# Mish in pieces on GpSimd, V scaled by one product there, two buffers for O, and a new order of the work, in a kernel that mixes attention with a feed-forward branch

## The chip, the core and the metric

The kernel runs on one core of a Trainium2 chip. The core has five engines that run independently and meet at semaphores: TensorE (PE, matrix products; PEld is its loading of weights), VectorE (DVE), ScalarE (ACT), GpSimd (POOL) and SyncE (SP, which only issues transfers here). Each engine works through its own list of instructions in order. The metric is the time on the device in microseconds (us); a measurement is the median of several runs.

## The reference

Two branches work on the same x of 2048 tokens and 640 features, all in bfloat16, and a gate mixes them:

```python
g = _sigmoid((x * gate_w).sum(-1, keepdims=True))
# A: 32 heads of 20, softmax over 2048 keys
p = _softmax(einsum("bhqd,bhkd->bhqk", q, k) * Dh ** -0.5)
a = einsum("bhqk,bhkd->bhqd", p, v) ... @ wo
# B: 640 -> 1536 -> 640 with Mish
h = einsum("bsd,df->bsf", x, w1) + b1
sp = log1p(exp(-abs(h))) + where(h > 0, h, 0)
b = einsum("bsf,fd->bsd", h * tanh(sp), w2)
return g * a + (1 - g) * b
```

The largest piece of elementwise work is the exponential of 32 x 2048 x 2048 scores.

## The kernel before

**Attention.** Heads are taken in 8 groups of 4 (their 20 dimensions padded to 32 partitions, so that four heads use the four row blocks of TensorE). Queries are taken in 4 chunks of 512, keys in 16 tiles of 128. A block is one head, one key tile and one query chunk: 128x512 scores, of which there are 2048. Scores come out with the keys on the partitions (`score_mms`, L1219), so that the exponentials can go straight into the product with V, which has a column of ones ahead of it for the sum (`pv`, L1456).

**Two engines make exponentials.** In each step ScalarE takes two blocks, or three when a bank of PSUM is spare, in one instruction (`emit_e`, L1246). Beside that VectorE takes whole tiles (four heads of one key tile, `emit_x`). For each of the four blocks one instruction scales the scores from PSUM into 16-bit integers that, read as float16, are an approximate exponential (L1304). Two more instructions add a constant to the whole 128x2048 tile (L1334), which gives two shifted copies, the shades. The product with V is then made three times, once with each shade, where the V of the second and third is scaled by 161/128 and 203/128. Those scaled V come from GpSimd: two products of 128x84 for each tile (`weigh`, L1359), kept in `VS`, which has 8 sets.

**End of a group of heads.** When all keys of a group and chunk are through, VectorE copies the accumulator to `OUNG` (L1551). SyncE moves the row of sums into `RR`, VectorE takes its reciprocal (L1558), SyncE writes it to DRAM and reads it back spread over the partitions into `BCT` (L1559, L1561), and GpSimd multiplies `OUNG` by `BCT` in four pieces of 128 columns (`times`, L1518). There is one `OUNG`.

**The feed-forward branch** runs between the steps of the attention as single tasks for TensorE (all through the helper `quarters`, L508): `h_task` makes x w1 (48 of them, VectorE adds the bias, L989), `mish` follows each second one (24 times, on 128x1024), `b_task` makes the product with w2, `p_task` that with wo. Mish is one Tanh on ScalarE (L1013), which gives U, and then six instructions on VectorE that compute a polynomial in U and multiply it by h:

```python
piece(FULL, lambda e: e.tensor_scalar(A, U, LIFT, LIFT, ALU.mult, ALU.add), taken)   # L1033
piece(SCALED, lambda e: e.tensor_scalar(B, A, 1 / LIFT, a - 2, ALU.mult, ALU.add))   # L1034
piece(FULL, lambda e: e.tensor_tensor(A, A, B, ALU.mult))                            # L1035
piece(SCALED, lambda e: e.tensor_scalar(B, A, 1 / LIFT, b - c, ALU.mult, ALU.add))   # L1036
piece(FULL, lambda e: e.tensor_tensor(A, A, B, ALU.mult))                            # L1037
piece(FULL, lambda e: e.tensor_tensor(h, A, h, ALU.mult), done)                      # L1038
```

U, A and B have one buffer each, so the next Mish waits for this one.

**What sets the order.** Nothing on the chip decides an order: a planner in Python (`Plan` and the loop at the end of `attention`) writes every engine's list when the kernel is built. It keeps an estimated time for each engine from constants in microseconds (`SHADE`, `TIMES`, `MISH` and others), emits one ScalarE step after the other, and fits the rest in: `start_tile` gives VectorE a new tile when VectorE is not too far behind, `pick` chooses a task for TensorE by its due step, `work` chooses the next instruction of VectorE from the queues `norm`, `soon` (shades), `blend` (Mish) and `bg`. Some twenty thresholds (`AHEAD`, `CROWD`, `XLATE`, `OVER` and others) steer this, and `STRETCHES` gives them other values for 35 stretches of steps. A transfer is taken as landed after an estimated time plus a margin (`safe`); GpSimd's products of O enter its list only then (`lasting`).

**The start.** SyncE loads the first chunk of x as rows, issues the transposing loads of chunks 1 and 2, then the three large blocks of wk, wq and wv, and then the transposing load of chunk 3.

Of the kernel before, what the change touches and what calls it, by code (L numbers as in the profile page):

```python
# [8 lines left out]
FP32 = mybir.dt.float32  # L9
# [8 lines left out]
P = 128  # L18
# [6 lines left out]
HG = 4  # L25
# [34 lines left out]
HALVED = 0.41  # L60
# [7 lines left out]
Q_WAIT = 6  # L68
# [7 lines left out]
TIMES = 0.7  # L76
# [13 lines left out]
MISH = 1.7  # L90
# [4 lines left out]
FULL = 0.60  # L95
SCALED = 0.34
LIFT = 512.0
FMIN = 0.109
# [12 lines left out]
CALM = 6  # L111
PACKED = 17
# [18 lines left out]
SETS = 8  # L131
ULPS = 1024 / math.log(2)
BASE = 13680.1
SHADE = 0.61
# [3 lines left out]
    13: {"EAGER": 144, "FMIN": 0.128, "FREE": 0.235, "SPUN": 0.495, "THIRD": 1.187, "VMIN": 1.48},  # L138
    33: {"EAGER": 144, "FMIN": 0.273, "FREE": 0.235, "SPUN": 0.495, "THIRD": 1.187, "VMIN": 1.48},
    53: {"CALLED": 7.573, "CALM": 3, "EAGER": 144, "FMIN": 0.332, "FREE": 0.235, "PATIENCE": 11.967, "ROOM": 2.116, "SPUN": 0.495, "THIRD": 1.187, "VMIN": 1.48, "XLATE": 10.107, "XSLACK": 0.076},  # L140
    74: {"AHEAD": 32, "CALLED": 7.573, "CALM": 8, "CROWD": 1.442, "EAGER": 144, "FMIN": 0.354, "FREE": 0.235, "NEED": 2, "OVER": 0.266, "PATIENCE": 3.941, "ROOM": 2.116, "SPUN": 0.467, "THIRD": 1.341, "VMIN": 1.48, "XLATE": 10.107, "XSLACK": 0.076},
    95: {"BUSY": 1.495, "CALLED": 2.701, "CROWD": 1.338, "FMIN": 0.33, "FREE": 0.173, "SPUN": 0.564, "STREAM": 0.496},
    116: {"CROWD": 1.454, "ROOM": 1.78, "STREAM": 0.464, "VMIN": 0.691, "XSLACK": 0.385},
    138: {"CROWD": 1.454, "EAGER": 159, "FREE": 0.15, "ROOM": 1.78, "STREAM": 0.464, "THIRD": 0.562, "VMIN": 0.691, "XSLACK": 0.385},
    159: {"XSLACK": 0.541},
    178: {"AHEAD": 13, "BEHIND": 21.412, "BUSY": 0.268, "CROWD": 1.246, "EAGER": 144, "FREE": 0.235, "MARGIN": 1.043, "OVER": 0.25, "PATIENCE": 12.851, "ROOM": 2.303, "XSLACK": 0.56},
    197: {"AHEAD": 17, "BEHIND": 13.21, "BUSY": 0.268, "CALLED": 2.332, "CALM": 9, "CROWD": 1.378, "EAGER": 144, "FMIN": 0.062, "FREE": 0.148, "LATER": 0.62, "MARGIN": 1.043, "OVER": 0.279, "PATIENCE": 8.968, "ROOM": 2.303, "XSLACK": 0.56},
    218: {"AHEAD": 17, "BEHIND": 13.21, "BUSY": 0.268, "CALLED": 2.332, "CALM": 9, "CROWD": 1.378, "EAGER": 156, "FMIN": 0.062, "FREE": 0.148, "KEPT": 14, "LATER": 0.62, "LOAD": 0.609, "MARGIN": 1.043, "OVER": 0.279, "PATIENCE": 13.444, "ROOM": 2.078, "STREAM": 0.365, "XLATE": 7.955, "XSLACK": 0.633},
    238: {"BUSY": 0.481, "EAGER": 131, "FMIN": 0.093, "LATER": 0.493, "LOAD": 0.49, "MARGIN": 0.871, "ROOM": 2.374, "XSLACK": 0.42},
    259: {"BUSY": 0.481, "CALLED": 1.571, "EAGER": 131, "FMIN": 0.065, "LATER": 0.493, "LOAD": 0.49, "MARGIN": 0.871, "NEED": 4, "OVER": 0.166, "ROOM": 2.345, "STREAM": 0.348, "VMIN": 2.036, "XSLACK": 0.42},  # L150
    279: {"AHEAD": 30, "BEHIND": 33.473, "BUSY": 0.531, "CALLED": 8.822, "CROWD": 1.719, "EAGER": 49, "FMIN": 0.065, "FREE": 0.217, "LATER": 0.531, "LOAD": 0.503, "MARGIN": 0.871, "NEED": 4, "OVER": 0.04, "ROOM": 2.185, "SLACK": 0.145, "SPARED": 1, "SPUN": 0.561, "STREAM": 0.574, "THIRD": 0.656, "VMIN": 2.036, "XSLACK": 0.539},
    301: {"AHEAD": 27, "BEHIND": 24.076, "BUSY": 0.655, "CALM": 8, "EAGER": 142, "FMIN": 0.157, "LATER": 0.445, "OVER": 0.136, "PATIENCE": 8.709, "ROOM": 3.21, "SLACK": 0.301},
    321: {"AHEAD": 27, "BEHIND": 24.076, "BUSY": 0.848, "CALM": 8, "EAGER": 125, "FMIN": 0.14, "FREE": 0.019, "LATER": 0.819, "MARGIN": 0.538, "OVER": 0.165, "PATIENCE": 7.178, "ROOM": 3.21, "SLACK": 0.301, "SPUN": 0.703, "THIRD": 0.853, "VMIN": 1.553, "XLATE": 6.963, "XSLACK": 0.575},
    343: {"OVER": 0.166},
    364: {},
    384: {"CALM": 5, "FREE": 0.144, "KEPT": 11, "OVER": 0.173, "XSLACK": 0.648},
    403: {"CALM": 5, "FREE": 0.072, "KEPT": 11, "OVER": 0.173, "SPARED": 2, "SPUN": 0.633, "XSLACK": 0.648},
    423: {"BEHIND": 10.627, "BUSY": 0.528, "CALLED": 3.206, "CALM": 5, "FREE": 0.072, "KEPT": 11, "MARGIN": 0.884, "OVER": 0.08, "PATIENCE": 6.789, "SPARED": 2, "SPUN": 0.633, "STREAM": 0.464, "XSLACK": 0.648},
    444: {"BUSY": 0.764, "CALLED": 6.746, "CALM": 5, "EAGER": 164, "FREE": 0.117, "MARGIN": -0.093, "OVER": 0.013, "THIRD": 1.182, "XLATE": 8.239},
    465: {"BEHIND": 11.273, "BUSY": 0.764, "CALLED": 6.746, "CALM": 5, "EAGER": 164, "FREE": 0.117, "LATER": 0.604, "MARGIN": -0.093, "OVER": 0.013, "ROOM": 1.536, "THIRD": 1.182, "VMIN": 0.904, "XLATE": 8.239},  # L160
    486: {"EAGER": 119, "OVER": 0.217, "SPARED": 2, "THIRD": 0.385},
    507: {"AHEAD": 48, "EAGER": 119, "OVER": 0.217, "SPARED": 1, "THIRD": 0.385, "VMIN": 1.003},
    527: {},
    546: {"OVER": 0.225, "ROOM": 1.348},
    566: {"BUSY": 1.219, "CALLED": 3.326, "FREE": 0.185, "LATER": 0.559, "LOAD": 0.591, "NEED": 4, "OVER": 0.225, "ROOM": 1.348, "SPUN": 0.456, "THIRD": 0.564},
    585: {"BUSY": 1.219, "CALLED": 2.639, "FREE": 0.185, "LATER": 0.559, "LOAD": 0.591, "NEED": 4, "OVER": 0.142, "ROOM": 1.696, "SLACK": 0.273, "SPUN": 0.533, "THIRD": 0.564, "XSLACK": 0.639},
    606: {"BUSY": 1.219, "CALLED": 2.639, "FREE": 0.185, "LATER": 0.559, "LOAD": 0.591, "NEED": 4, "OVER": 0.142, "PATIENCE": 3.342, "ROOM": 1.696, "SLACK": 0.273, "SPUN": 0.533, "THIRD": 0.564, "VMIN": 1.96, "XSLACK": 0.639},
    626: {"AHEAD": 23, "CALLED": 7.432, "OVER": 0.276, "PATIENCE": 13.247},
    646: {"AHEAD": 20, "CALLED": 0.719, "CROWD": 1.213, "EAGER": 131, "KEPT": 11, "LOAD": 0.617, "MARGIN": -0.47, "PATIENCE": 7.296, "ROOM": 3.379, "SPUN": 0.491, "THIRD": 0.632, "VMIN": 1.391, "XLATE": 8.962},
    668: {"AHEAD": 20, "CALLED": 0.719, "CROWD": 1.213, "EAGER": 131, "KEPT": 11, "LOAD": 0.619, "MARGIN": -0.47, "OVER": 0.152, "PATIENCE": 7.296, "ROOM": 3.379, "SPUN": 0.681, "THIRD": 0.632, "VMIN": 1.391, "XLATE": 7.539},  # L170
    690: {"AHEAD": 20, "CALLED": 3.772, "CROWD": 1.085, "EAGER": 127, "KEPT": 11, "LOAD": 0.619, "MARGIN": -0.5, "OVER": 0.152, "PATIENCE": 7.296, "ROOM": 3.379, "SPUN": 0.681, "THIRD": 0.632, "VMIN": 1.391, "XLATE": 7.539},
    709: {},
}
USUAL = {name: globals()[name] for some in STRETCHES.values() for name in some}


# [1830 lines left out]
```

## Time and profile before

| | |
|---|---|
| median of 3 runs | 752.74 us (752.46 to 753.23) |
| the profiled execution | 752.22 us, of which the span from the first to the last instruction is 750.3 us |
| granted TensorE clock | 0.997 |
| busy: PE, DVE, ACT, POOL | 721.5, 689.9, 732.8, 211.8 us |
| first exponential starts, last one ends | 8.2 us, 741.2 us |
| blocks on ScalarE, on VectorE | 1540 (659 pairs, 74 triples), 508 (127 tiles) |

Busy time is the time in which at least one instruction of an engine was under way. Instructions of one engine overlap at their ends, so that the sum over groups is more than the busy time; the distance from start to start says what one more instruction costs. An idle time is put down to what ended it. A wait of an engine with nothing else to do costs nothing.

### The profile page before, as it was taken

The page shows a single profiled execution, that of the slowest core. Times are in us where ns is not written, and L with a number is a line of the kernel's source. Part 1 is how long each engine was busy: PE and PEld are TensorE (multiplying, and loading weights), DVE is VectorE, ACT ScalarE, POOL GpSimd, SP SyncE. Part 2 cuts the span into 40 slices and gives each one's busy share as a digit, 9 for nine tenths or more (in the row PEclk, how much of TensorE's full clock was granted, in tenths as well). Part 3 has the DMA queues.
Part 4 walks back from the last instruction along what each step waited for, and adds up shares of the span by engine and source line. Part 5 has one row for each costly group of instructions (what it writes and reads, how often), then busy time and mean ns, then how long its engine had stood idle before and what let it go on. Part 6 is the DMA issues. An engine that isn't in the chain of part 4 may idle for free.

```text
span 750.3 us, 25694 instructions
## 1 busy us (share of the span) xinstructions
PE 721.5 (96%) x11307; PEld 274.8 (37%) x11307; DVE 689.9 (92%) x1203; ACT 732.8 (98%) x764; POOL 211.8 (28%) x399
## 2 busy tenths in 40 slices
PE   8899999999999999999989999999999999999996
PEld 3333334334423342233333433334444434333342
DVE  3698898999999999998999999999999999999986
ACT  6899999999999999999999999999999999999995
POOL 3203241312332213232213332212331243313142
PEclk9999999999999999999999999999999999999998
DMA  9402422132233313632132111111212212010001
GB/s 235 61 26 70 83 85 85 26 112 64 57 93 119 94 56 88 181 70 54 41 86 74 56 34 30 43 43 56 87 52 70 68 58 70 21 30 21 30 17 42
DMA packets 78015, 50.44 MB, mean 67 GB/s; under 512 B 21408, under 2 KB 73880, under 8 KB 77848
## 3 DMA queue, kind: packets, MB, share of 16 engines
q1 hardware_dynamic: 75528, 48.24, 23.3%
q8 instruction: 91, 1.49, 0.9%
q10 hardware_dynamic: 2256, 0.47, 0.3%
q14 instruction: 28, 0.23, 0.1%
q0 software_dynamic: 112, 0.01, 0.1%
HBM read 39.01 MB, written 8.90 MB: 64 GB/s over the span
## 4 chain that ended last, share of the span: by engine, by line
ACT 63%; PE 18%; DVE 11%; DMA 4%; SPq 1%; issue 1%; POOL 0%; DVEq 0%
ACT ETS L1246 62%; PE PS L508 6%; PE PS L1219 6%; PE PS L1456 5%; DVE LN L1304 3%; DVE LN L1334 2%; DMA XB<-in_A_x_dram 2%; SPq L557 1%; ACT REG L1013 1%; DMA W2R<-in_B_w_dram 1%; DMA BCT<-SUMS 1%; DVE REG L1304 1%; DVE HB L989 1%; DMA RR<-OUNG 1%; ACT W2R L1013 1%
## 5 line engine op out<-in xcount | busy, mean ns | idle before, releaser
L1246 ACT ACTIVATE ETS<-PS 128x1024 bf16<-128x1024 f32 (+1 forms) x733 | 711.2, 1158 | 3.8 <-PE PS L1219 3.1
L1219 PE MATMUL PS<-QT,KT 32*128 32x512 bf16 (+1 forms) x2128 | 287.6, 377 | 14.0 <-ACT ETS L1246 10.5
L1304 DVE TENSOR_SCALAR LN<-PS 128x512 int16<-128x512 f32 x396 | 266.1, 682 | 25.0 <-PE PS L1219 23.6
L1518 POOL TENSOR_TENSOR QT<-OUNG,BCT 128x128 bf16<-128x128 f32 x124 | 65.9, 562 | 481.6 <-DMA BCT<-SUMS 481.6
L1219 PEld LDWEIGHTS PS<-QT,KT 32*128 32x128 bf16 x2128 | 72.3, 91 | 238.9 <-ACT ETS L1246 211.5
L1359 POOL TENSOR_SCALAR VS<-V_all 128x84 bf16<-128x84 bf16 x262 | 138.9, 530 | 35.9 <-DVE V_all L836 8.0
L1456 PE MATMUL PS<-ETS,V_all 128*21 128x512 bf16 (+1 forms) x1596 | 148.0, 375 | 0.1
L1334 DVE TENSOR_SCALAR LN<-LN 128x2048 int16<-128x2048 int16 x182 | 126.1, 695 | 3.7 <-PE PS L1456 3.1
L508 PE MATMUL PS<-XB,REG 128*32 128x256 bf16 (+2 forms) x1800 | 87.2, 296 | 2.7 <-DVE LN L1304 1.8
L1456 PE MATMUL PS<-LN,VS 128*21 128x512 f16 (+1 forms) x832 | 78.7, 379 | 0.3
L508 PE MATMUL PS<-W2R,HB 128*32 128x320 bf16 x1536 | 74.4, 301 | 0.0
L1456 PEld LDWEIGHTS PS<-ETS,V_all 128*21 128x21 bf16 x1596 | 37.8, 90 | 50.4 <-issue 42.2
L508 PEld LDWEIGHTS PS<-XB,REG 128*32 128x32 bf16 (+1 forms) x1800 | 41.7, 96 | 29.9 <-issue 19.4
L508 PE MATMUL PS<-WOQ,QT 128*32 128x320 bf16 x1024 | 50.7, 301 | 0.6 <-DVE QT L1544 0.5
L508 PEld LDWEIGHTS PS<-W2R,HB 128*32 128x32 bf16 x1536 | 35.8, 96 | 24.2 <-issue 12.2
L1304 DVE TENSOR_SCALAR REG<-PS 128x512 int16<-128x512 f32 x60 | 40.1, 679 | 1.5 <-PE PS L1219 1.2
L1456 PE MATMUL PS<-LN,V_all 128*21 128x512 f16 (+1 forms) x408 | 38.7, 376 | 0.2 <-DVE OUNG L1551 0.2
L508 PE MATMUL PS<-XB,WOQ 128*32 128x512 bf16 (+2 forms) x440 | 35.5, 382 | 0.3 <-DVE LN L1304 0.3
L1456 PEld LDWEIGHTS PS<-LN,VS 128*21 128x21 bf16 x832 | 19.7, 89 | 39.9 <-issue 21.6
L989 DVE TENSOR_TENSOR HB<-PS,B1F 128x512 bf16<-128x512 f32 x48 | 32.6, 679 | 0.5 <-PE PS L508 0.4
L508 PEld LDWEIGHTS PS<-WOQ,QT 128*32 128x32 bf16 x1024 | 23.2, 96 | 17.3 <-issue 8.7
L1304 DVE TENSOR_SCALAR W2R<-PS 128x512 int16<-128x512 f32 x36 | 24.2, 682 | 0.6 <-PE PS L1219 0.6
(116 smaller groups left out, 496.8 us busy)
## 6 DMA issues: line engine op xcount, KB each, us to landing
REG<-in_B_w_dram SPq DMA_DIRECT2D x36, 320.0 KB, 3.3
BCT<-SUMS SPq DMA_DIRECT2D x31, 256.0 KB
W2R<-in_B_w_dram SPq DMA_DIRECT2D x12, 320.0 KB, 4.2
QT<-QS SPq DMA_DIRECT2D x28, 128.0 KB, 3.3
KT<-KS SPq DMA_DIRECT2D x28, 128.0 KB
KS<-LN SPq DMA_DIRECT2D x16, 128.0 KB, 3.4
QS<-WOQ SPq DMA_DIRECT2D x16, 120.0 KB
W2R<-in_B_w_dram SPq DMA_DIRECT2D x12, 160.0 KB, 3.8
```

Source lines behind the costliest of these rows:

```text
L508: last = e.matmul(to[at + j:at + j + n, :], w[:, j:j + n], x, start=start, stop=stop, tile_position=(0, at + j))
L557: "sp", lambda e: e.dma_start_transpose(xt(c), x_ap[c * CW:(c + 1) * CW, :]), (), f"xt{c}", cost=4.5, tail=3.6)]
L989: ev = dve(lambda e: e.tensor_tensor(hb, PS[:, bank, :].rearrange("p (i t) -> p i t", i=2), bias, ALU.add), [last, *b1f, *guarded, *b_read ...
L1013: ex = pl.add("act", lambda e: e.activation(U, h, AF.Tanh, bias=BEND, scale=0.5), [ev, u_free[0]], cost=0.94)
L1219: op = pl.add("pe", lambda e, to=to, g=real(g), tile=tile, j=j, cols=cols, c=c, of_q=of_q: e.matmul(to[:, cols], KT[32 * j:32 * j + 32, g, ...
L1246: e_op[s] = pl.add("act", lambda e: e.activation(RING[:, p:p + n, :], scores(s)[:, 0:n, :], AF.Exp, scale=SCALE), [s_op[s], *(pv_slot[b] f ...
L1304: bank_free[bank] = x_ops[bank] = tile["op"] = dve(lambda e: e.tensor_scalar(dst, PS[:, bank, :], SCALE * ULPS, BASE, ALU.mult, ALU.add), ...
L1334: op = pl.add("dve", lambda e: e.tensor_scalar(to, src, SHADES[n] - SHADES[held], None, ALU.add), [made, *deps], cost=SHADE)
L1359: weighted[(c, g, k)] = n, [pl.add("pool", lambda e, i=i, n=n, src=src: e.tensor_scalar(VS[:, n, i, :, :], src, WEIGHTS[i + 1], None, ALU. ...
L1456: lasts[n] = pl.add("pe", lambda e, v=v, j=j, src=src[:, cols], of_q=of_q, begin=begin, end=end: e.matmul(PS[32 * j:32 * j + EW, ACC, of_q ...
L1518: oung_free[0] = bc_read[0] = otn_done[(c, g)] = pl.add("pool", lambda e, some=some: e.tensor_tensor(otn(c, g)[:, some], src[:, some], BC[ ...
```

## The change

Four things are changed in the instructions, and the planner with them.

1. Mish's first instruction and its three products go to GpSimd, in pieces of 256 columns, so 16 instructions there in place of 4 on VectorE. The two instructions that scale and shift (L1034, L1036) stay on VectorE, whole. The chain alternates: GpSimd (4 pieces), VectorE, GpSimd (4), VectorE, GpSimd (8). Chains follow one another; a piece enters GpSimd's list in `grind`, at each step, when by the plan it is ready and GpSimd is not far ahead.
2. V is scaled by one product of 2 x 84 columns, with a constant tensor `SCALES` (filled at the start by two fills on GpSimd) and V read twice by a stride of zero. `VS` has 5 sets in place of 8.
3. `OUNG` has two buffers, used in turn. The products of O enter GpSimd's list 2.0 us after the planned landing of `BCT` (`HANG`) and no longer at the planned landing and a margin of 5.6 us.
4. At the start the transposing load of chunk 3 stands ahead of the three blocks of weights. Some small tensors (`GT1`, `MXS`, `MXR`, `FLAG`) share storage with others.

The planner gets other estimates (for a piece of the first instruction 0.43 us, for one of a product 0.69, for V's product 0.65, for O's products 0.45 in place of 0.7, for a shade 0.64 in place of 0.61, for two copies and some transfers longer ones), and `STRETCHES` is rewritten: again 35 stretches, with other values, and the last one begins at step 716 in place of 709. So the order of the instructions is another one throughout.

```diff
-TIMES = 0.7
+TIMES = 0.45
...
-SETS = 8
+SETS = 5
...
-SHADE = 0.61
+SHADE = 0.64
...
-    OUNG = sb("OUNG", [P, CW], FP32)
+    OUNG = sb("OUNG", [P, 2, CW], FP32)
+    SCALES = sb("SCALES", [P, len(SHADES) - 1, HG * EW], BF16)
...
-            load_x(1)
-            load_x(2)
+            for c in range(1, NC):
+                load_x(c)
...
-            load_x(3)
...
+            m_scales.extend(pl.add("pool", lambda e, i=i: e.memset(SCALES[:, i, :], WEIGHTS[i + 1]), cost=0.2)
+                            for i in range(len(SHADES) - 1))
...
-                piece(FULL, lambda e: e.tensor_scalar(A, U, LIFT, LIFT, ALU.mult, ALU.add), taken)
-                piece(SCALED, lambda e: e.tensor_scalar(B, A, 1 / LIFT, a - 2, ALU.mult, ALU.add))
-                piece(FULL, lambda e: e.tensor_tensor(A, A, B, ALU.mult))
-                piece(SCALED, lambda e: e.tensor_scalar(B, A, 1 / LIFT, b - c, ALU.mult, ALU.add))
-                piece(FULL, lambda e: e.tensor_tensor(A, A, B, ALU.mult))
-                piece(FULL, lambda e: e.tensor_tensor(h, A, h, ALU.mult), done)
...
+                lift = lambda e, at: e.tensor_scalar(A[:, at], U[:, at], LIFT, LIFT, ALU.mult, ALU.add)
+                times = lambda e, at: e.tensor_tensor(A[:, at], A[:, at], B[:, at], ALU.mult)
+                last = lambda e, at: e.tensor_tensor(h[:, at], A[:, at], h[:, at], ALU.mult)
...
+                chains.append((ex, due, [
+                    ("pool", HW, LIFTED, lift, taken), ("dve", 2 * CW, SCALED, plus(a - 2), None), ("pool", STONE, MILLED, times, None),
+                    ("dve", 2 * CW, SCALED, plus(b - c), None), ("pool", STONE, MILLED, times, None), ("pool", STONE, MILLED, last, done)]))
...
+            def grind():
+                while mill and mill[0][0].t1 + HOP < pl.now["act"] + AWAY and pl.now["pool"] < pl.now["act"] + GRIST:
+                    mill.popleft()[1]()
...
-                weighted[(c, g, k)] = n, [pl.add("pool", lambda e, i=i, n=n, src=src: e.tensor_scalar(
-                    VS[:, n, i, :, :], src, WEIGHTS[i + 1], None, ALU.mult), [v_done[(real(g), k)], m_one, was], cost=0.58)
-                    for i in range(len(SHADES) - 1)]
+                both = VS[:, n, :, :, :].rearrange("p i j c -> p i (j c)")
+                one = src.rearrange("p j c -> p (j c)").unsqueeze(1).to_broadcast([P, len(SHADES) - 1, HG * EW])
+                op = pl.add("pool", lambda e, both=both, one=one: e.tensor_tensor(both, one, SCALES[:, :, :], ALU.mult), [
+                    v_done[(real(g), k)], m_one, was, *m_scales], cost=WEIGH)
...
-            ev = dve(lambda e: e.tensor_copy(src, PS[:, ACC, :]), [last, oung_free[0]], WIDE)
+            ev = dve(lambda e: e.tensor_copy(src, PS[:, ACC, :]), [last, oung_free[m]], WIDE)
...
-            if lasting and (safe(lasting[0][0]) < pl.now["act"] or step not in slots):
+            if lasting and (lasting[0][0].t1 + HANG < pl.now["act"] or step not in slots):
```

More of the change, by code (lines that the diff above doesn't have):

```diff
@@ new lines, in onward, with run @@
+            def onward(op, n):
+                ex, due, steps = chains[0]
+                if n == len(steps):
+                    chains.popleft()
+                    if chains:
+                        onward(chains[0][0], 0)
+                    return
+                eng, w, cost, fn, after = steps[n]
+                count = 2 * CW // w
+                def run(i):
+                    some = slice(i * w, (i + 1) * w)
+                    got = pl.add(eng, lambda e: fn(e, some), [op, *read], cost=cost)
+                    if i == count - 1:
+                        if after:
+                            after(got)
+                        onward(got, n + 1)
+                if eng == "dve":
+                    blend.append((cost, lambda: run(0), lambda: op, due))
+                else:
+                    mill.extend((op, lambda i=i: run(i)) for i in range(count))
```

162 lines of the change are left out of this document (87 added, 75 removed).

## The prediction

> **What bounds the kernel now.** I read the page's busy times first, then the busy time of each engine by stage, the groups of instructions, the waits, and last the timeline at single places.
>
> ```profile
> PE 721.5 (96%) x11307; PEld 274.8 (37%) x11307; DVE 689.9 (92%) x1203; ACT 732.8 (98%) x764; POOL 211.8 (28%) x399
> ...
> L1246 ACT ACTIVATE ETS<-PS 128x1024 bf16<-128x1024 f32 (+1 forms) x733 | 711.2, 1158 | 3.8 <-PE PS L1219 3.1
> ```
> ```profile
> 0.00:50.00 50.00, 43.97 (x621) 17.45 (x621) 31.00 (x57) 42.07 (x47) 12.01 (x24) 1.00 0.54 112
> 50.00:150.00 100.00, 97.72 (x1258) 37.24 (x1258) 88.34 (x148) 100.00 (x103) 29.10 (x58) 1.00 0.26 70
> 150.00:650.00 500.00, 488.45 (x7882) 186.35 (x7873) 480.63 (x842) 499.02 (x521) 138.86 (x257) 1.00 0.25 70
> 650.00:700.00 50.00, 49.82 (x771) 16.76 (x772) 48.18 (x83) 49.91 (x55) 19.35 (x36) 1.00 0.08 23
> 700.00:750.30 50.30, 41.51 (x798) 16.96 (x790) 41.74 (x76) 41.75 (x43) 12.43 (x25) 0.95 0.11 31
> ```
>
> (Columns of the second: PE, PEld, DVE, ACT, POOL.) From 50 to 700 us ACT is never idle, and it waits 3.8 us in all before its exponentials. The time is therefore ACT's work plus the two ends. VectorE is the second bound: 96% in 150 to 650, the stage that holds Mish. The two share the exponentials, so a microsecond freed on VectorE shortens the kernel only if the planner turns it into more tiles there. GpSimd has 72% of that stage free.
>
> ```profile
> L1246 ACT ACTIVATE ETS<-PS 128x1024 bf16<-128x1024 f32 x659 | 624.8, 1115 | 3.0 <-PE PS L1219 2.2 <-PE PS L1456 0.2
> L1246 ACT ACTIVATE ETS<-PS 128x1536 bf16<-128x1536 f32 x74 | 113.1, 1540 | 0.9 <-PE PS L1219 0.9
> ```
> ```profile
> 358.56 0.68 DVE L1334 TENSOR_SCALAR LN<-LN 128x2048 int16<-128x2048 int16 x1
> 359.16 1.28 DVE L1304 TENSOR_SCALAR LN<-PS 128x512 int16<-128x512 f32 x2
> 360.36 0.68 DVE L1334 TENSOR_SCALAR LN<-LN 128x2048 int16<-128x2048 int16 x1
> ...
> 365.28 0.69 DVE L1304 TENSOR_SCALAR LN<-PS 128x512 int16<-128x512 f32 x1
> 365.88 0.69 DVE L1033 TENSOR_SCALAR U<-REG 128x1024 f16<-128x1024 f32 x1
> 366.48 0.55 DVE L1052 TENSOR_SCALAR XB<-PS,OMG 128x320 bf16<-128x320 f32 x1
> ```
>
> **The exchange rate.** ACT handles 659 x 2 + 74 x 3 = 1540 blocks of 128x512, so one costs 711.2 / 1540 = 0.462 us and a tile (four blocks) 1.85. VectorE's instructions overlap at their ends; what counts is start to start, 0.60 us for an L1304, an L1334 and an L1033 alike. A tile there is four L1304 and two L1334, 3.60 us; with the L1334 that wait, 3.63. If VectorE is freed by D and the end moves forward by x, then x / 1.85 more tiles need 3.63 x / 1.85 = D - x, so **x = D / 2.96**.
>
> **What leaves VectorE.**
>
> ```profile
> L1033 DVE TENSOR_SCALAR U<-REG 128x1024 f16<-128x1024 f32 x18 | 12.3, 682 | 0.0
> ...
> L1035 DVE TENSOR_TENSOR U<-U 128x1024 f16<-128x1024 f16 x24 | 16.5, 690 | 0.0
> L1038 DVE TENSOR_TENSOR HB<-U,HB 128x1024 bf16<-128x1024 f16 x24 | 16.4, 682 | 0.0
> L1037 DVE TENSOR_TENSOR U<-U 128x1024 f16<-128x1024 f16 x24 | 16.3, 680 | 0.0
> ...
> L1036 DVE TENSOR_SCALAR U<-U 128x1024 f16<-128x1024 f16 x24 | 10.3, 428 | 0.2
> ```
>
> Of Mish's six instructions the first and the three products go, 24 times each: 96 x 0.60 = **57.6 us**. L1034 and L1036 stay. With no cost anywhere x would be 57.6 / 2.96 = 19.5 us.
>
> **What GpSimd takes on.** Each Mish becomes 4 + 12 instructions of 256 columns. The trace has none; the nearest rows, alone and undisturbed, are these:
>
> ```profile
> L1518 POOL TENSOR_TENSOR QT<-OUNG,BCT x124: 447/457/1178, 57.0 to 733.6; 128x128 bf16<-128x128 f32 x124
> ```
> ```profile
> L1359 POOL TENSOR_SCALAR VS<-V_all x262: 417/418/1441, 17.3 to 735.7; 128x84 bf16<-128x84 bf16 x131
> ```
> ```profile
> L1874 POOL TENSOR_TENSOR HB<-LN,W2R 128x320 bf16<-128x320 f32 x1 | 0.9, 857 | 7.8 <-ACT LN L1872 7.8
> ...
> L591 POOL COPY WOQ<-WOQ 128x400 bf16<-128x400 bf16 x1 | 0.5, 517 | 3.5 <-DMA WOQ<-in_A_wqkv_dram 3.5
> ```
>
> (The numbers after the count in the first two are minimum, median, maximum ns.) Two inputs: 457 ns at 128 columns and 857 at 320, so 2.08 ns a column and 724 at 256; bounds 457 and 857; I take 0.70 from start to start. One input: between 418 and 517; I take 0.45. A Mish is 4 x 0.45 + 12 x 0.70 = 10.2 us, all 24 are 245. V's two products become one of 168 columns, 0.457 + 40 x 0.0021 = 0.54, for 262 / 2 = 131 tiles: 71 us instead of 262 x 0.418 = 110. The products of O stay at 57 us. In 150 to 650 that is 245 + (71 + 57) x 500 / 700 = 336 us, a load of 67% where 28% is shown, before any disturbance. None of it is on ACT's path as long as it is done in time.
>
> **What they do to each other.** At 601.75 an L1334 begins while GpSimd multiplies, and takes 0.95 us where 0.68 is usual:
>
> ```profile
> 601.75 0.95 DVE L1334 TENSOR_SCALAR LN<-LN 128x2048 int16<-128x2048 int16 x1
> ```
> ```profile
> 601.65 2.19 POOL L1518 TENSOR_TENSOR QT<-OUNG,BCT 128x128 bf16<-128x128 f32 x4 [14.59 <-DMA BCT<-SUMS]
> ```
>
> Four such products alone are 1.7 us; these took 2.19. So each makes the other wait. Now the price for the 230 instructions of VectorE in this stage that behave so (about 182 L1334, 48 of L1034 and L1036). Below: the L1334 cost 0.015 us more on average than the 0.68 of a quiet one, with GpSimd 28% busy; at 67% that is 230 x 0.015 x 67 / 28 = 8 us.
>
> ```profile
> L1334 DVE TENSOR_SCALAR LN<-LN 128x2048 int16<-128x2048 int16 x182 | 126.1, 695 | 3.7 <-PE PS L1456 3.1
> ```
>
> Above: GpSimd began 0.10 us before the L1334, had 0.36 left, and 0.27 were lost, so about 0.1 of a remaining wait is free. Someone who comes at a random point of a 0.72 us product then loses (0.62 x 0.62 / 2) / 0.72 = 0.27 at worst, at 67%: 230 x 0.67 x 0.27 = 41 us. The same reckoning for today's rows (0.44 us long; 110 + 57 us of 700, or 24%, busy without the waits) gives 254 x 0.24 x 0.13 = 8 us where 254 x 0.015 = 4 are seen; it overstates by two, so I take 20, of which 3 are paid today: **17 us**. D = 57.6 - 17 = 40.6 and x = **13.7 us**, some seven tiles.
>
> The Trainium skill states the rule behind this (SBUF — State Buffer, § Who interferes with whom): GpSimd and a two-port VectorE instruction exclude each other for the whole instruction. The 0.95 us above agrees. Its page Perfetto Trace Analysis (§ Optimizing Scalar/DVE Operations) concludes that moving work between these two might not help; by that the sum would be near zero, and that is a rival below.
>
> **TensorE** gets three passes instead of one and separate scores for seven tiles, under 1 us each. It hides them in its waits for ACT; without that cover they cost up to 6 us.
>
> ```profile
> POOL QT L1518 <- DMA BCT<-SUMS: 481.6, 31, 28.0
> PEld PS L1219 <- ACT ETS L1246: 211.5, 583, 1.3
> ...
> DVE OUNG L1551 <- POOL QT L1518: 0.8, 1, 0.8
> ```
>
> **Smaller edits.** The second buffer for O removes at most that 0.8 us. Loading the fourth chunk of x ahead of the three weight blocks: SP sits 9.21 us on that transpose behind them, and ACT has gaps of 1.03 and 0.86 us soon after. I take 1 us (0 to 1.9). The weights start one transpose later, some 4 us (the first two took 8.24); their first use is due at step 40. The two new fills on GpSimd fall into its empty first 20 us. Fewer V sets (5 for 8) only shorten GpSimd's lead. Merged small tensors change no instruction.
>
> ```profile
> 1.75 8.24 SPq L557 DMA_TRANSPOSE XB<-in_A_x_dram  x2
> ...
> 12.03 9.21 SPq L557 DMA_TRANSPOSE XB<-in_A_x_dram  x1
> ```
> ```profile
> 25.95 5.96 ACT L1246 ACTIVATE ETS<-PS 128x1024 bf16<-128x1024 f32 x6 [1.03 <-PE PS L1219]
> 32.77 1.45 ACT L1246 ACTIVATE ETS<-PS 128x1536 bf16<-128x1536 f32 x1 [0.86 <-PE PS L1219]
> ```
>
> **New waits.** GpSimd works in order, so Mish pieces and V products stand behind O's products, which wait for their transfer; behind the Mish pieces stand VectorE's L1034 and L1036 and then TensorE's second feed-forward product. I allow 3 us (0 to 8) for TensorE coming too early. **Sum:** the profiled execution is 752.2 us (span 750.3 and 1.9 around it); 752.2 - 13.7 - 1 + 3 = 740.5. The median of the runs lies 0.5 higher: **741 us**.
>
> **Rivals.** (1) Little contention: only the 8 us, D = 53, x = 18, no stalls: 752.7 - 18 - 1 = **734**. For it: most L1334 show 0.68. (2) The lock takes most: 41 us, D = 20, x = 7, and 3 lost: **748**. This is the skill's warning as a mechanism. (3) The freed time is not used, since TensorE is busy 98% and its banks are taken: **752**, the start's 1 us apart. Against it are the 211.5 us it waits for ACT. (4) Slower: GpSimd becomes the bound. Each of the 230 also delays it by about 0.45 us at 67%: 336 + 69 = 405 us of 500. The waits for O's transfer, 31 x 500 / 700 = 22 in the stage, are harmless up to 95 / 22 = 4.3 us each; today they are 15.5 on average, only because nothing stands behind them. At 5 us the stage is 515 long, and the gain falls away too: 752.7 + 15 - 1 = **767**, less if the planner spreads Mish: say **760**.
>
> **How the numbers follow.** Forecast (737 to 745) 0.40; rival 1, 0.15; rival 2, 0.20; rival 3, 0.10; rival 4, 0.15. A measurement tells 0.2%, 1.5 us, from no change. Faster is the first three, 0.75; same 0.10; slower 0.15. The range 732 to 753 leaves out rival 4 and a twentieth below.
>
> **What would show it.** Right: POOL near 400 us busy, VectorE still above 95% in the stage, some seven tiles more (L1304 from 508 to about 536, ACT's blocks down by the same number), L1334 means near 0.75 us, ACT still full. Rival 1: L1334 below 0.72. Rival 2: above 0.8. Rival 3: VectorE falls below 92%. Rival 4: TensorE or ACT wait for HB or VS from GpSimd. The prediction is wrong if ACT shows idle time in the stage, or the tiles do not increase.

## The result and the profile after

| | before | after |
|---|---|---|
| median of 5 runs each, same chip | 752.65 us (751.34 to 753.23) | 759.65 us (755.75 to 759.97) |
| span of the profiled execution | 750.3 us | 758.1 us |
| blocks on ScalarE | 1540 | 1512 |
| busy: PE, DVE, ACT, POOL | 721.5, 689.9, 732.8, 211.8 us | 731.4, 683.7, 726.3, 405.1 us |

The change makes the kernel slower: the ratio of the means is 1.0079, with a 95% interval of 1.0051 to 1.0108 (all ratios below are of means too). The five runs after go with TensorE's granted clock: 755.75 us at 0.999, 756.95 at 0.996, and 759.65 to 759.97 in the three at 0.993, of which the profiled execution is one. The prediction was 741 us, in a range of 732 to 753, with 0.75 on faster. It was wrong in sign, and the time lies outside its range.

The busy times and the costliest groups of the kernel after, from its page:

```profile
PE 731.4 (96%) x11356; PEld 278.5 (37%) x11356; DVE 683.7 (90%) x1149; ACT 726.3 (96%) x762; POOL 405.1 (53%) x660
...
L1285 ACT ACTIVATE ETS<-PS 128x1024 bf16<-128x1024 f32 (+1 forms) x731 | 703.6, 1106 | 13.2 <-PE PS L1258 10.1
...
L1038 POOL TENSOR_TENSOR U<-U 128x256 f16<-128x256 f16 x192 | 144.0, 777 | 68.2 <-DVE U L1042 68.2
L1373 DVE TENSOR_SCALAR LN<-LN 128x2048 int16<-128x2048 int16 x195 | 154.0, 793 | 6.7 <-PE PS L1497 6.0
```

ScalarE's work fell, from 711.2 to 703.6 us of exponentials, as it was meant to. But its idle time ahead of them rose from 3.8 to 13.2 us. A shade (before L1334, after L1373) takes 793 ns on average instead of 695. The busy times by stage, in the same stretches as before (columns PE, PEld, DVE, ACT, POOL, the clock):

```profile
0.00:50.00 50.00, 45.95 (x621) 18.86 (x621) 31.34 (x57) 41.60 (x47) 9.74 (x20) 1.00 0.55 112
50.00:150.00 100.00, 99.57 (x1294) 37.36 (x1286) 87.55 (x152) 100.00 (x104) 16.82 (x37) 1.00 0.27 72
150.00:650.00 500.00, 486.95 (x7637) 180.86 (x7625) 474.54 (x789) 491.05 (x516) 313.40 (x501) 0.99 0.24 68
650.00:700.00 50.00, 48.46 (x807) 18.24 (x799) 48.93 (x81) 48.68 (x52) 42.91 (x68) 1.00 0.13 36
700.00:758.10 58.10, 50.48 (x1027) 23.21 (x1025) 41.31 (x76) 44.99 (x47) 22.21 (x36) 0.97 0.11 32
```

In 150 to 650 us ScalarE was full (499.02 of 500). Now it is idle for 9 us there.

**Where the 7.8 us of span are.** The exponentials by shape say how much work is left on ScalarE:

```profile
L1285 ACT ACTIVATE ETS<-PS 128x1024 bf16<-128x1024 f32 x681 | 644.4, 1076 | 11.6 <-PE PS L1258 8.5 <-PE PS L1497 0.8
L1285 ACT ACTIVATE ETS<-PS 128x1536 bf16<-128x1536 f32 x50 | 75.6, 1518 | 1.6 <-PE PS L1258 1.6
```

681 x 2 + 50 x 3 = 1512 blocks, so 2048 - 1512 = 536 are on VectorE, 134 tiles instead of 127. The median distance from one exponential to the next is 0.904 us for a pair and 1.330 for a triple, in both kernels. Whatever a distance is longer than that I call wait below, summed over all exponentials in the trace. (It is more than the idle time, since an exponential that waits for nothing starts 0.2 us before the one ahead of it ends.)

| term | before | after | difference |
|---|---|---|---|
| exponentials alone: pairs x 0.904 + triples x 1.330 | 694.2 | 682.1 | -12.1 |
| first exponential starts, and waits of the first 100 us | 8.2 + 4.7 | 9.9 + 2.9 | -0.1 |
| waits after 100 us | 11.0 | 27.5 | **+16.5** |
| from the last exponential to the end | 9.05 | 12.54 | **+3.5** |
| sum | | | +7.8 |

The rest of the span, 23 us in both, is almost all Mish's 24 Tanh on ScalarE. The gain came as forecast, and waits of ScalarE that were not there before ate it. What they follow, by the waits of after and then of before (us in total, times, longest):

```profile
PEld PS L1258 <- ACT ETS L1285: 181.2, 503, 1.2
...
PEld PS L1497 <- DVE LN L1373: 23.1, 70, 0.9
```
```profile
PEld PS L1219 <- ACT ETS L1246: 211.5, 583, 1.3
...
PEld PS L1456 <- DVE LN L1334: 11.0, 44, 0.5
```

TensorE waits twice as long for shades, 23.1 us instead of 11.0, and 30 us less for ScalarE: it comes earlier less often. One such place in the timeline of after (start, duration, engine, line, idle time before and what ended it):

```profile
434.43 3.45 POOL L1039 TENSOR_TENSOR HB<-U,HB 128x256 bf16<-128x256 f16 x4
434.45 1.20 DVE L1373 TENSOR_SCALAR LN<-LN 128x2048 int16<-128x2048 int16 x1
...
435.70 0.10 PEld L1497 LDWEIGHTS PS<-LN,VS 128*21 128x21 bf16 x4 [0.67 <-DVE LN L1373]
...
436.17 1.18 DVE L1373 TENSOR_SCALAR LN<-LN 128x2048 int16<-128x2048 int16 x1
...
437.40 0.10 PEld L1497 LDWEIGHTS PS<-LN,VS 128*21 128x21 bf16 x4 [0.68 <-DVE LN L1373]
...
438.37 1.02 ACT L1285 ACTIVATE ETS<-PS 128x1024 bf16<-128x1024 f32 x1 [0.89 <-PE PS L1258]
```

Two shades begin while GpSimd multiplies, and take 1.20 and 1.18 us. TensorE works through its list in order: the product with V that needs the shade (L1497) waits 0.67 and 0.68 us, and behind it stand scores for ScalarE (L1258). At 438.37 ScalarE has stood idle for 0.89 us.

### The profile page after: what moved, and what is told of

It reads as the page before. It is cut to its first block, busy times and chain, and to the rows that moved or that the text cites. A ratio compares the mean times of both kernels' runs of the same rounds, so it can differ in the third digit from the quotient of the medians.

```text
span 758.1 us, 25947 instructions
## 1 busy us (share of the span) xinstructions
PE 731.4 (96%) x11356; PEld 278.5 (37%) x11356; DVE 683.7 (90%) x1149; ACT 726.3 (96%) x762; POOL 405.1 (53%) x660
## 4 chain that ended last, share of the span: by engine, by line
PE 45%; ACT 26%; DVE 24%; POOL 2%; issue 1%; DMA 0%
ACT ETS L1285 26%; PE PS L516 15%; PE PS L1258 15%; PE PS L1497 13%; DVE LN L1343 8%; DVE LN L1373 7%; PE PS L864 2%; DVE HB L999 1%; DVE REG L1343 1%; PE PS L604 1%; DVE U L1042 1%; DVE REG L1373 1%; POOL U L1038 1%; DVE OUNG L1594 1%; POOL HB L1039 1%
## 5 line engine op out<-in xcount | busy, mean ns | idle before, releaser
L1285 ACT ACTIVATE ETS<-PS 128x1024 bf16<-128x1024 f32 (+1 forms) x731 | 703.6, 1106 | 13.2 <-PE PS L1258 10.1
L1343 DVE TENSOR_SCALAR LN<-PS 128x512 int16<-128x512 f32 x420 | 280.0, 680 | 26.9 <-PE PS L1258 25.6
L1258 PE MATMUL PS<-QT,KT 32*128 32x512 bf16 (+1 forms) x2133 | 290.4, 379 | 8.7 <-ACT ETS L1285 6.3
L1038 POOL TENSOR_TENSOR U<-U 128x256 f16<-128x256 f16 x192 | 144.0, 777 | 68.2 <-DVE U L1042 68.2
L1373 DVE TENSOR_SCALAR LN<-LN 128x2048 int16<-128x2048 int16 x195 | 154.0, 793 | 6.7 <-PE PS L1497 6.0
L1258 PEld LDWEIGHTS PS<-QT,KT 32*128 32x128 bf16 x2133 | 73.5, 91 | 233.7 <-ACT ETS L1285 181.2
L1497 PE MATMUL PS<-ETS,V_all 128*21 128x512 bf16 (+1 forms) x1572 | 146.4, 376 | 0.0
L1559 POOL TENSOR_TENSOR QT<-OUNG,BCT 128x128 bf16<-128x128 f32 x124 | 59.4, 508 | 119.0 <-DMA BCT<-SUMS 119.0
L1400 POOL TENSOR_TENSOR VS<-V_all,SCALES 128x168 bf16<-128x168 bf16 x137 | 79.4, 589 | 60.3 <-PE PS L1497 47.3
L516 PE MATMUL PS<-XB,REG 128*32 128x256 bf16 (+1 forms) x1800 | 89.5, 298 | 1.7 <-DVE HB L999 1.3
L1497 PE MATMUL PS<-LN,VS 128*21 128x512 f16 (+1 forms) x880 | 84.5, 382 | 5.9 <-DVE LN L1373 4.2
L1039 POOL TENSOR_TENSOR HB<-U,HB 128x256 bf16<-128x256 f16 x96 | 73.9, 792 | 1.6
L1497 PEld LDWEIGHTS PS<-ETS,V_all 128*21 128x21 bf16 x1572 | 37.7, 90 | 47.5 <-issue 40.0
L1037 POOL TENSOR_SCALAR U<-REG 128x256 f16<-128x256 f32 x72 | 35.3, 512 | 34.5 <-ACT REG L1023 33.2
L516 PEld LDWEIGHTS PS<-XB,REG 128*32 128x32 bf16 x1800 | 41.8, 96 | 30.1 <-issue 19.6
L1497 PE MATMUL PS<-LN,V_all 128*21 128x512 f16 (+1 forms) x432 | 41.4, 379 | 0.0
L1497 PEld LDWEIGHTS PS<-LN,VS 128*21 128x21 bf16 x880 | 21.2, 89 | 50.7 <-DVE LN L1373 22.5
```

Source lines behind the costliest of these rows:

```text
L516: last = e.matmul(to[at + j:at + j + n, :], w[:, j:j + n], x, start=start, stop=stop, tile_position=(0, at + j))
L1037: lift = lambda e, at: e.tensor_scalar(A[:, at], U[:, at], LIFT, LIFT, ALU.mult, ALU.add)
L1038: times = lambda e, at: e.tensor_tensor(A[:, at], A[:, at], B[:, at], ALU.mult)
L1039: last = lambda e, at: e.tensor_tensor(h[:, at], A[:, at], h[:, at], ALU.mult)
L1258: op = pl.add("pe", lambda e, to=to, g=real(g), tile=tile, j=j, cols=cols, c=c, of_q=of_q: e.matmul(to[:, cols], KT[32 * j:32 * j + 32, g, ...
L1285: e_op[s] = pl.add("act", lambda e: e.activation(RING[:, p:p + n, :], scores(s)[:, 0:n, :], AF.Exp, scale=SCALE), [s_op[s], *(pv_slot[b] f ...
```

## The experiments

Two theories. **Theory 1, exclusion:** GpSimd's pieces hold up VectorE's shades, the shades hold up TensorE's list, and that holds up ScalarE. **Theory 2, lateness:** GpSimd's own results come late, and whoever needs them waits. Beside these stand the new order itself and the smaller edits. All runs were timed beside the kernel before, whose median was 751.5 to 752.7 us throughout. In the first four the lists of TensorE, VectorE and ScalarE are the very ones of the changed kernel.

**GpSimd's Mish work almost taken away.** Each piece computes 8 of its 256 columns (the rest of Mish is left out); order and waits stay.

```diff
-                    some = slice(i * w, (i + 1) * w)
+                    some = slice(i * w, i * w + (8 if eng == "pool" else w))
```

> The order of every engine's list and all waits are those of the changed kernel; only each of Mish's 16 pieces on GpSimd works on 8 of its 256 columns (the rest of Mish is left out, and its buffers are filled once at the start). Theory 1 (exclusion: VectorE's shades wait behind GpSimd's pieces, and TensorE behind the shades): mean of a shade back to 0.70 us from 0.79, the waits ahead of the exponentials from 30 us to about 16, the time from 759.7 to 743 to 747. Theory 2 (GpSimd's chain of 24 us is late for its readers): the same fall here. Theory 3 (the new order is worse in itself, whatever GpSimd takes): the time stays at 757 to 760.

Measured: 743.54 us (741.81 to 743.85), a ratio of 0.9878 [0.9858, 0.9897]. From its groups of instructions, Mish's products on POOL and the shades on DVE (count, busy us, mean ns, idle time ahead):

```profile
L1041 POOL TENSOR_TENSOR U<-U 128x8 f16<-128x8 f16 x192 | 40.4, 239 | 191.8 <-DVE U L1045 191.8
```
```profile
L1376 DVE TENSOR_SCALAR LN<-LN 128x2048 int16<-128x2048 int16 x195 | 138.1, 711 | 9.0 <-PE PS L1500 8.1
```

The whole loss comes with GpSimd's Mish work: without it, the same order is 9 us faster than before. The terms agree. The exponentials alone are 682.1 us again, the waits after 100 us fall from 27.5 to 11.9, and only the longer end stays (12.2 us), so the end belongs to the new order: ScalarE's last instruction waits for TensorE for 5.6 us in both, where it was 2.5 in the kernel before.

**Half of it.** Pieces of 128 columns in the same place (the other half of Mish is left out).

```diff
-                    some = slice(i * w, (i + 1) * w)
+                    some = slice(i * w, i * w + (128 if eng == "pool" else w))
```

> The changed kernel in its own order, each of GpSimd's Mish pieces computing 128 of its 256 columns (the other half of Mish is left out). GpSimd's Mish work beyond the other duties was 78 us with 8 columns (743.5 us) and 267 us in full (759.65 us); with pieces of 128 columns it should be about 167 us, since the run with each piece split in two had (472 - 138)/2 = 167 us per such set. Theory 1, the loss grows with the time in which GpSimd shuts VectorE out of memory: 743.5 + 16.1 x (167 - 78)/(267 - 78) = 751 us (749 to 753.5), waits ahead of the exponentials near 22 us (14.7 and 30.4 at the ends). Theory 2, the order has slack that swallows the first delays and the loss comes all at once when results arrive late: 747 us or less, waits under 18 us.

Measured: 746.13 us (744.98 to 746.55), 0.9917 [0.9904, 0.9931]. The same two groups of this run:

```profile
L1041 POOL TENSOR_TENSOR U<-U 128x128 f16<-128x128 f16 x192 | 89.9, 496 | 129.1 <-DVE U L1045 129.1
```
```profile
L1376 DVE TENSOR_SCALAR LN<-LN 128x2048 int16<-128x2048 int16 x195 | 142.1, 732 | 8.1 <-PE PS L1500 7.3
```

Half of the work costs a sixth of the loss: 2.6 of 16.1 us. The straight line that I had drawn for theory 1 is wrong. The shades say why. Over the 711 ns of the run before they lose 21 ns, while with whole pieces they lose 82: a piece that is half as long is met half as often, and the one who meets it waits half as long. A quarter of 16.1 would be 4.0 us. That only 2.6 came may be slack in the order, since VectorE is busy only 469.5 of 500 us in the stage with the tiny pieces; no run shows that alone. The time is the one that theory 2 had forecast (747 or less), and the waits, about 20 us, lie between the two forecasts. So this run doesn't choose between the theories; the next one does.

**Exclusion without readers.** The pieces have full size, but work on a buffer of their own, and nobody waits for them (most of Mish is left out).

```diff
-                lift = lambda e, at: e.tensor_scalar(A[:, at], U[:, at], LIFT, LIFT, ALU.mult, ALU.add)
-                times = lambda e, at: e.tensor_tensor(A[:, at], A[:, at], B[:, at], ALU.mult)
-                last = lambda e, at: e.tensor_tensor(h[:, at], A[:, at], h[:, at], ALU.mult)
+                lift = lambda e, at: e.tensor_scalar(A[:, at], A[:, at], 0.25, 0.25, ALU.mult, ALU.add)
+                times = lambda e, at: e.tensor_tensor(A[:, at], A[:, at], A[:, at], ALU.mult)
+                last = times
...
+        for op in self.ops:
+            if op.free or op.eng in ("act", "pe", "sp"):
+                deps = list(op.deps)
+                while any(d.ghost for d in deps):
+                    deps = list(dict.fromkeys(x for d in deps for x in (d.deps if d.ghost else [d])))
```

> GpSimd's pieces keep their size and place and still wait for what they waited for, but they multiply a buffer with itself that nobody reads, and neither VectorE nor ScalarE nor TensorE waits for them (most of Mish is left out). Theory 1 (exclusion): shades stay at 0.78 to 0.80 us, waits ahead of the exponentials stay at 26 to 32 us, time 755 to 760. Theory 2 (lateness): shades stay, but the time falls as in the kernel with small pieces, to 750 or less. Theory 3 (order): 757 to 760.

Measured: 755.15 us (753.79 to 757.32), 1.0041 [1.0027, 1.0055]. The shades among its groups of DVE:

```profile
L1386 DVE TENSOR_SCALAR LN<-LN 128x2048 int16<-128x2048 int16 x195 | 150.4, 774 | 6.9 <-PE PS L1510 5.9
```

This splits the loss. From tiny pieces to pieces without readers the time rises by 755.15 - 743.54 = 11.6 us, although nobody waits for GpSimd's Mish: that is exclusion, the larger part. From there to the changed kernel it rises by 4.5 by the medians, by 2.9 by the ratios, whose intervals overlap a little. In the traces the waits after 100 us are 11.9, 22.6 and 27.5 us in the three.

The last step is not lateness alone. The pieces without readers also disturb less: their shades lose 25.8 us, those of the changed kernel 28.6 (table below). And the trace of after has two stretches with TensorE's clock at half (last section), where the other two have none before their ends. The run with the old order of loads (below) has the same lists of TensorE, VectorE, ScalarE and GpSimd as the changed kernel, and no such stretch between 30 us and its end; there the waits after 100 us are about 24 us. What waits for Mish's results in the trace of after is little, by its waits and by the row of the scaling instructions:

```profile
PEld PS L516 <- POOL HB L1039: 0.7, 1, 0.7
...
PE PS L516 <- POOL HB L1039: 0.4, 1, 0.4
```
```profile
L1042 DVE TENSOR_SCALAR U<-U 128x1024 f16<-128x1024 f16 x48 | 20.9, 436 | 0.0
```

TensorE waits 1.1 us, VectorE not at all. Lateness may be worth anything from about 1 us to 4.5 in the changed kernel; its size isn't shown.

**Each piece in two.** Twice as many pieces of 128 columns, all of Mish computed.

```diff
-                    got = pl.add(eng, lambda e: fn(e, some), [op, *read], cost=cost)
+                    def both(e):
+                        if eng == "pool":
+                            fn(e, slice(i * w, i * w + w // 2))
+                            return fn(e, slice(i * w + w // 2, (i + 1) * w))
+                        return fn(e, some)
+                    got = pl.add(eng, both, [op, *read], cost=cost)
```

> Each piece on GpSimd is issued as two instructions of 128 columns in its place: 384 more instructions, about 0.14 us more for each product, 40 us more of GpSimd, but a shade that comes waits for half as long. Theory 1: mean of a shade from 0.79 to about 0.74 us, time 2 to 5 us below the changed kernel. Theory 2: a Mish takes 26 to 28 us in place of 24, and the time is the same or up to 4 us above. Theory 3: no change.

Measured: 778.56 us (776.22 to 781.89), 1.0345 [1.0318, 1.0372], far more than exclusion explains. Shades and Mish's scaling among its groups of DVE, then a row of its waits (us in total, times, longest):

```profile
L1378 DVE TENSOR_SCALAR LN<-LN 128x2048 int16<-128x2048 int16 x195 | 147.6, 760 | 7.6 <-PE PS L1502 6.8
...
L1042 DVE TENSOR_SCALAR U<-U 128x1024 f16<-128x1024 f16 x48 | 25.3, 527 | 15.5 <-POOL U L1037 12.5 <-POOL U L1038 2.8
```
```profile
ACT ETS L1290 <- PE PS L1263: 28.5, 37, 3.1
```

The shades do lose less (760 ns instead of 793), but GpSimd is busy 472 us instead of 405 for the same work, and falls behind its plan. VectorE then stands at the scaling instructions L1042 for 12.5 + 2.8 us, with shades and blocks queued behind them. That is theory 2, at far more than the 4 us that it had allowed: lateness is cheap while GpSimd keeps its plan (4.5 us at most) and dear when it doesn't. How much of the 19 us it is can't be told exactly, since TensorE's clock is at half for 30.7 us between 258 and 733 us of this trace. So exclusion and lateness pull the length of a piece in opposite directions.

The shades that took over 0.72 us, summed from each trace over the 0.684 us of a quiet one, put these runs in one row:

| run | delayed shades | time lost on them | median of the runs |
|---|---|---|---|
| tiny pieces | 39 of 268 | 7.2 us | 743.5 us |
| half a piece | 66 | 12.7 us | 746.1 us |
| full pieces, no readers | 99 | 25.8 us | 755.2 us |
| the changed kernel | 114 | 28.6 us | 759.7 us |
| pieces in two | 104 | 18.5 us | 778.6 us |

The kernel before has 28 of 254, and 3.4 us. The tiny pieces still lose 7.2 although hardly anything of Mish is left on GpSimd; V's single product, which the kernel before doesn't have, is part of that (5.0 us in a run below that adds it alone).

**The planner told what the trace shows.** Durations from the trace of after, the same thresholds, a new order.

```diff
-LIFTED = 0.43
-MILLED = 0.69
+LIFTED = 0.475
+MILLED = 0.74
...
-SHADE = 0.64
-WEIGH = 0.65
+SHADE = 0.72
+WEIGH = 0.54
```

> The planner is told what the trace of the changed kernel shows from start to start: a shade 0.72 us (was 0.64), a piece of a product 0.74 (0.69), of the first instruction 0.475 (0.43), V's product 0.54 (0.65); it plans anew with the same thresholds. If the loss is that real work comes later than planned, waits ahead of the exponentials fall from 30 us to 18 to 24 and VectorE gets a few tiles less (130 to 133 in place of 134): time 749 to 756. If the thresholds matter more than the costs, the waits stay at 28 or more: 757 to 763.

Measured: 765.44 us (763.29 to 766.38), 1.0168 [1.0155, 1.0181]. Its exponentials by shape:

```profile
L1285 ACT ACTIVATE ETS<-PS 128x1024 bf16<-128x1024 f32 x653 | 618.6, 1085 | 6.5 <-PE PS L1497 3.0 <-PE PS L1258 2.3
L1285 ACT ACTIVATE ETS<-PS 128x1536 bf16<-128x1536 f32 x82 | 123.4, 1509 | 2.5 <-PE PS L1258 2.4
```

The time lies above both ranges that were expected. The idle time falls from 13.2 to 9.0 us, which fits the first case: a plan that knows of late shades leaves room for them. But 653 x 2 + 82 x 3 = 1552 blocks stay on ScalarE, 40 more than after, worth 40 x 0.462 = 18 us. The thresholds in `STRETCHES` were written for the other estimates, and with new ones the planner starts ten tiles fewer.

**All four back on VectorE, and wider pieces.** Both change the estimates, so both are planned anew with thresholds that were not made for them.

```diff
-                    ("pool", HW, LIFTED, lift, taken), ("dve", 2 * CW, SCALED, plus(a - 2), None), ("pool", STONE, MILLED, times, None),
-                    ("dve", 2 * CW, SCALED, plus(b - c), None), ("pool", STONE, MILLED, times, None), ("pool", STONE, MILLED, last, done)]))
+                    ("dve", 2 * CW, 0.60, lift, taken), ("dve", 2 * CW, SCALED, plus(a - 2), None), ("dve", 2 * CW, 0.60, times, None),
+                    ("dve", 2 * CW, SCALED, plus(b - c), None), ("dve", 2 * CW, 0.60, times, None), ("dve", 2 * CW, 0.60, last, done)]))
```

> Mish's first instruction and its products are on VectorE again, whole, as before; the rest of the change (V by one product, two buffers for O, load order, costs, thresholds) stays, and the planner plans anew with it. VectorE is loaded with 58 us more, so about seven tiles go back to ACT (127); shades 0.69 to 0.70 us, waits ahead of the exponentials about 16. If Mish on GpSimd is the whole of the loss, the time is 751 to 755, the kernel before within its noise; if other parts of the change or thresholds that do not suit cost something, 756 to 762.

Measured: 793.63 us (787.16 to 795.62), 1.0535 [1.0504, 1.0565], with 120 tiles.

```diff
-MILLED = 0.69
-STONE = 256
+MILLED = 1.38
+STONE = 512
...
-                    ("pool", HW, LIFTED, lift, taken), ("dve", 2 * CW, SCALED, plus(a - 2), None), ("pool", STONE, MILLED, times, None),
+                    ("pool", CW, 2 * LIFTED, lift, taken), ("dve", 2 * CW, SCALED, plus(a - 2), None), ("pool", STONE, MILLED, times, None),
```

> Pieces of 512 columns for 256 (estimates doubled): half as many instructions, about 22 us less for GpSimd, but a shade that comes waits for up to 1.2 us. If the length of a piece governs (exclusion), shades rise from 0.79 to 0.85 us or more and the time rises by 3 to 8 us. If GpSimd's lateness governs, as the 19 us of the kernel with halves suggest, the time falls by 2 to 6 us, although the shades are longer.

Measured: 768.90 us (768.49 to 769.95), 1.0220 [1.0207, 1.0233], with 128 tiles and shades of 829 ns. The shades lengthen with the pieces as theory 1 has it. Of the times neither says anything on Mish: with Mish on VectorE the kernel before needs 752.7 and this one 793.6, so thresholds that don't fit, with what else of the change is left in, are worth 40 us. Both runs are inconclusive.

**The order of the loads.** The fourth chunk of x again behind the weights.

```diff
-            for c in range(1, NC):
-                load_x(c)
+            load_x(1)
+            load_x(2)
...
+            load_x(3)
```

> The transposing load of chunk 3 of x stands behind the three blocks of weights again; nothing else. If the load order is worth what was forecast, ACT has its gap of 1 us near 26 us again and the time is 0.5 to 2 us above the changed kernel. If the later first exponential (9.9 us in place of 8.2 in the profiled execution) comes from the load order, it is back at 8.2 and the time is 1 to 2 us below; if it comes from when TensorE's full clock is granted, it changes from execution to execution without regard to this edit.

Measured: 758.21 us (756.19 to 759.3), 1.0072 [1.0053, 1.0092]. In time that is not told from the changed kernel's 1.0079. In the profiled executions the start to 100 us (first exponential and waits) is 8.2 + 6.5 us here and 9.9 + 2.9 after. That difference of 1.9 us is not the loads' alone. ScalarE's gap near 26 us is back, 1.37 us long, but TensorE's clock is also at half for 3.41 us from 25.96 on. And the first exponential does not follow the loads: it starts at 8.2 us in the run with half pieces, which has the new order of loads, and at 10.0 in the run with five sets below, which has the old one. So what the order of loads is worth stays open.

**V by one product.** In the kernel before, first with five sets, then five sets alone, then one product with all eight. Every other engine keeps its list of before.

```diff
-SETS = 8
+SETS = 5
...
-                weighted[(c, g, k)] = n, [pl.add("pool", lambda e, i=i, n=n, src=src: e.tensor_scalar(
-                    VS[:, n, i, :, :], src, WEIGHTS[i + 1], None, ALU.mult), [v_done[(real(g), k)], m_one, was], cost=0.58)
-                    for i in range(len(SHADES) - 1)]
+                op = pl.add("pool", lambda e, both=both, one=one: e.tensor_tensor(both, one, SCALES[:, :, :], ALU.mult), [
+                    v_done[(real(g), k)], m_one, was, *m_scales], cost=0.65)
```

> The kernel before with one part of the change alone: V scaled by one product of 2 x 84 columns into 5 sets, for two products into 8. GpSimd's busy time falls from 212 us to about 160; nothing waits for it in either. The time is that of the kernel before within 1 us (751.5 to 753.5).

> The kernel before with five sets of scaled V in place of eight, V still scaled by two products, every engine's order as before. The run with five sets and one product was 755.2 us, 2.8 us above before. Theory A, five sets make the scaled V late, since GpSimd then waits for TensorE to be done with a set (218 us in 44 waits there): 755 us (754 to 756). Theory B, the two-input product itself disturbs VectorE: 752.4 us, within 0.7.

> The kernel before with V scaled by one product and all eight sets, every engine's order as before. Theory A, lateness by the five sets: 752.4 us, within 0.7. Theory B, the two-input product disturbs VectorE's shades: 755 us (754 to 756), shades longer than the 698 ns of before, waits ahead of the exponentials near 19 us.

Measured: one product and five sets 755.21 us (754.7 to 756.16), 1.0040 [1.0028, 1.0053]; five sets alone 752.05 us, 1.0004 [0.9993, 1.0014]; one product and eight sets 755.02 us (754.56 to 755.08), 1.0038 [1.0025, 1.0052]. From the groups of POOL, the product in the last of these, and what it replaced in the kernel before:

```profile
L1365 POOL TENSOR_TENSOR VS<-V_all,SCALES 128x168 bf16<-128x168 bf16 x131 | 74.2, 595 | 15.4 <-DVE V_all L840 8.2 <-DVE W2R L1308 7.2
```
```profile
L1359 POOL TENSOR_SCALAR VS<-V_all 128x84 bf16<-128x84 bf16 x262 | 138.9, 530 | 35.9 <-DVE V_all L836 8.0 <-DVE W2R L1304 7.2
```

Fewer sets cost nothing. The single product, which frees 65 us of an engine that had time to spare, costs 3 us in that order. Delayed shades carry only 5.0 - 3.4 = 1.6 us of it (VectorE is busy 693.0 us instead of 689.9). How the rest comes about stays open.

No run that computes all of Mish beat the kernel before.

## Why the prediction was wrong

**Right: the gain.** Seven tiles more were forecast, L1304 from 508 to about 536: it is 536. 13.7 us less of ScalarE's work were forecast; 12.1 were measured. But that it came so close is luck, for the step to it was not sound. I deducted the exclusion from what VectorE can spend on tiles. The planner had spent it before anything ran: it wrote 134 tiles and put only 0.03 us more on a shade, 268 x 0.03 = 8 us in all.

**Right: the prices on GpSimd.** 0.70 us for a product and 0.45 for the first instruction were taken; alone they take 0.67 and 0.40 in the trace of after. About 400 us of busy time were named as the sign, and 405.1 came out.

**Nearly right: the exclusion on VectorE.** 20 us of VectorE were taken for the stage, between bounds of 8 and 41; the shades lose 22.8 us there (1.8 before), and 28.6 in the whole kernel (3.4 before). The 48 instructions of L1034 and L1036, which I had counted with them, are hardly met: 436 ns in after, 418 with the tiny pieces. The Trainium skill's rule (SBUF — State Buffer, § Who interferes with whom), that GpSimd and a two-port VectorE instruction shut each other out for the whole instruction, is borne out: all 114 delayed shades had to wait for the end of a GpSimd instruction. The Trainium skill's page Perfetto Trace Analysis (§ Optimizing Scalar/DVE Operations) warned that moving work between these two might not help, and it did not help.

**The step that failed is "New waits", where I allowed 3 us (0 to 8).** It measured 16.5 us after the first 100, and 3.5 more at the end. I looked only for those who wait for GpSimd's results; that part is 4.5 us at most. I had not asked what a late shade holds up. The order on TensorE is fixed, scores for ScalarE stand behind the product that waits for the shade, and so the exclusion is paid as idle time of the engine that sets the end: 11.6 us with nobody waiting for GpSimd's Mish. Some 3 of the 16.5 us go with the two stretches at half the clock; the run with the old order of loads has about 24 us of waits without them. The run with tiny pieces gives the sum as it would have been without: 743.5 us, where 741 was forecast.

**The rivals.** Rival 4 gave 760 us, which is the time that came out, but for another reason: GpSimd did not become the bound. It is busy 313 of 500 us in the stage, not 405, and TensorE waits 1.1 us in all for Mish's results. The split pieces are the only run that looks like rival 4. Rival 2 had the mechanism, exclusion, but priced it in tiles and so stopped at 748. The sign that I had set against the forecast, idle time of ScalarE in the stage, is what came.

**Smaller terms.** 1 us for the order of the loads isn't seen in the time, and no run shows what it is worth. V's single product was counted as a relief of GpSimd and nothing else; in the order of before it costs 3 us. The longer end, 3.5 us, was in no term: the new order leaves ScalarE's last instruction waiting 5.6 us for TensorE instead of 2.5.

## What to carry to other kernels

When work moves to an engine that shuts another out of memory, price it in two places: the time that the other loses, and, where orders are fixed when the kernel is built, what stands behind each delayed instruction on the way to the engine that sets the end. In this kernel the second was the one that was paid: the tiles came as planned, and the idle time with them. The price grows faster than the work, since a longer instruction is met more often and holds longer, but cutting it up can cost the moved work its punctuality. Estimates and thresholds of a planner belong together: to change the estimates alone cost 6 us more in one run here, and hid the effect that was to be measured in two others.

## What the runs showed of the hardware

**The exclusion has a fixed pattern.** In the trace of after, all 114 delayed shades began in a GpSimd instruction with 0.17 us or more left, and end 0.545 to 0.555 us after that instruction does; with half pieces it is 0.546 to 0.553 for all 66. A quiet shade takes 0.684, so the first 0.135 us of such a wait are free, and the rest is lost whole. Thirteen more began with over 0.2 us left and were not delayed: all of them started within 0.033 us of GpSimd's instruction, and then it was that one which took longer, 0.95 to 1.24 us. So GpSimd pays too: its product of 256 columns takes 0.67 us where no shade is near it and 0.87 on average where one is.

**TensorE's clock falls to half for a few microseconds.** In the profiled execution of after, the granted clock is 0.50 for two stretches of 3.41 us, one of which is here (columns as above, the clock behind POOL):

```profile
310.00:313.89 3.89, 2.77 (x35) 0.75 (x34) 3.69 (x6) 3.89 (x4) 0.00 (x0) 1.00 0.83 261
313.89:317.30 3.41, 3.41 (x31) 0.62 (x27) 3.00 (x5) 2.69 (x4) 0.48 (x1) 0.50 0.53 144
317.30:320.00 2.70, 2.20 (x35) 0.52 (x27) 2.30 (x4) 2.06 (x2) 0.48 (x1) 1.00 0.70 211
```

TensorE was busy 2.77 of 3.89 us ahead of it, then fully busy at half speed, and ScalarE lost 0.7 us in it. The trace of the kernel before has no such stretch between its start and its end; that of the run with one product and eight sets, with the same lists but GpSimd's, has two. That waits bring them about is argued from the order in time, and what they cost from the runs' clocks and times in the result; no run here tested either alone.
